# Sparse attention into a gated feed-forward layer: a new order in the lead-in, smaller weight loads, a finer first output stage and paired scores

## The chip, the cores and the metric

The kernel runs on one core of one Trainium2 chip. The metric is the time of one execution on the device in microseconds (us); where several executions were measured, their median. Each profile shows one execution. Its engines are TensorE (PE for matrix products, PEld for the loads of their stationary operand), VectorE (DVE), ScalarE (ACT), GpSimd (POOL) and SyncE (SP); the last two issue nearly all DMA transfers.

## What is computed

Attention over 4 batches, 8 heads, 768 positions and 64 dimensions. Each query sees the keys closer than 16 positions, and a maximum of the keys over each block of 32; the values of a block are averaged. The result, as 3072 rows of 512, goes through a feed-forward layer of width 2048.

```python
k_sum = k.reshape(B, H, nb, block, D).max(axis=3)        # block = 32
v_sum = v.reshape(B, H, nb, block, D).mean(axis=3)
scores_l = scale * q @ k.T,  masked to |i - j| < 16
scores_s = scale * q @ k_sum.T + log(block)
a = softmax(concatenate([scores_l, scores_s]))
x = (a @ concatenate([v, v_sum])).transpose(0, 2, 1, 3).reshape(3072, 512)
h = x @ w_in                                             # 512 x 2048
out = (h * sigmoid(1.702 * h)) @ w_out                   # 2048 x 512
```

## The kernel before, in words

**Units of work.** A batch is cut into two halves of 384 positions (`HALF`), a half into three stripes of 128 (`JH`). Heads go in pairs, numbered 0 to 3, so that a pair fills 128 partitions; two pairs form a group g. The feed-forward width is cut into 16 tiles of 128 (`NT`), numbered nt.

**Order.** Every engine executes its instructions in the order in which the program writes them (class `_Ordered`, lines 18 to 32). The order is written out by hand: in the lead-in as a list of calls (lines 895 to 1027), later as plans that say which piece of attention stands behind which slot of the feed-forward work. All instructions go through line 28, so the profile gives all of them that line; they are told apart by the names of the tiles.

**Lead-in** (lines 926 to 1005). Batch 0, first half, pair by pair. `k_turn` and `q_turn` transpose on TensorE (banks ps_k, ps_q); `k_max` takes the block maxima on DVE (ks); `s_bias`, `s_own`, `s_edges` make the scores (ps_s), `s_exp` their exponentials on ACT (a_sb). `b_turn(g)` makes the scores of the blocks for group g (ps_b, in two halves of two pairs of matmuls) from ks, `b_exp` their exponentials (ab). `v_sum(p)` sums the values of blocks (ps_vt), `v_copy` brings the sums to memory (vs). `av_own`, `av_edges` and `av_blocks` multiply with the values (ps_av), `v_norm` divides on DVE (rc, x), `x_turn` transposes the result (ps_x), `x_copy` copies it (xT), and `ff_first(p)` adds pair p's part to the first two tiles of the feed-forward layer (ph, lines 855 to 865). `gelu_soon` and `exp_soon` are one-element activations that make ACT load its table early.

**Loads** (lines 897 to 918, 1027). POOL issues them in the order of the program: queries, keys, values of batch 0, then w_in in five pieces of columns (256, 256, 512, 512, 512), w_out tiles 0 to 3, the late half of the queries (`load_q1`, four DMAs), w_out tiles 4 to 7 and 8 to 11, the masks (`finish_masks`, computed on POOL itself), w_out tiles 12 to 15, and then batch 1. At most eight DMAs of this queue are under way: an issue waits for the landing of the one eight places ahead of it.

**First output stage** (lines 1092 to 1099). `ff_out(0, ms, part)` multiplies stripe ms of the first half with four tiles of w_out (po). The twelve slots run over the four parts outside and the three stripes inside, so that a part of w_out is used by all stripes before the next is needed. Behind the slots, `plan0` (line 1030) puts the second half's attention of batch 0: q0 to q3 (`q_late`: transpose of the late queries of a pair into a bank, copy on DVE), s0 to s3 (`scores`, followed at once by `mask` on DVE), v0 and v1 (`values` of a group), x0 and x1 (`tx`, transpose and copy of the results). Behind slots 10 and 11, `w_sum(0)` and `w_sum(1)` make sums of w_out on DVE that later batches use. 

**Second half of batch 0, and batch 1.** `ff_in(1, ...)` with `todo` (line 1101) beside it: transposes of batch 1's keys (`tk`) and queries (`tq`), `w_sum(2)` and `w_sum(3)`, and `value_rows(1)` (block sums of batch 1's values, ps_vs). Then `ff_out(1, ms, part)` (line 1112, stripes outside, parts inside) with `plan1` (line 1032) beside it: t2, t3 (`tq`), s and m with half and pair (`scores`, `mask`), v with half and group, x with half and group, g (`gelu_soon`). Scores use the banks psb (two), values of batch 1, transposed queries, po and ph the banks pmm (four). Batches 2 and 3 follow plan `plan` beside sums and products of a fast matrix product (`product`, `g_sums`; poA, poB, poC).

**Last batch** (lines 1170 to 1221). Its feed-forward layer uses the same kind of fast product: `ff_do` runs seven products (1 to 7), copies (a, s, b, c) and gelus (A, B, C, E) for each j by the table `steps`, seven slots per j. Four tiles are computed plainly (`plain`). Banks: A three, B one, C two, E two. `x_sums` and `g_sums` are sums on DVE and POOL that the products use.

Of the kernel before, what the change touches and what calls it, by code (L numbers as in the profile page):

```python
# [10 lines left out]
BF16 = mybir.dt.bfloat16  # L11
# [24 lines left out]
def kernel(  # L36
# [225 lines left out]
    def load_w_out(c):  # L262
        wo = moe_w_out.rearrange("(nt ni) d -> ni nt d", ni=128)
        pool.dma_start(out=w_out_sb[:, c * 4:(c + 1) * 4, :],
                       in_=wo[:, c * 4:(c + 1) * 4, :])
# [151 lines left out]
    def q_late(p, eng):  # L417
        if p < 2:
            ps = psb.tile([128, 2048], BF16, name="ps_q", tag="big")
        else:  # L420
            ps = pmm.tile([128, 1024], BF16, name="ps_q", tag="mm")
        turn_plain(ps[:, 0:HALF], qb2["late"][:, 2 * p:2 * p + 2])
        copy(eng, qT[p][0][:, HALF:S].rearrange("p (c r) -> p c r", r=JH),
             ps[:, 0:HALF].rearrange("p (r c) -> p c r", r=JH))
# [206 lines left out]
    def tx(half, g):  # L631
        ps = psb.tile([128, 2, HALF], F16, name="ps_x", tag="big")
        for i in range(2):
            for j in range(JH):
                pe.transpose(out=ps[:, i, j * 128:(j + 1) * 128],
                             in_=x2[g][:, i, j].rearrange("p h d -> p (h d)"), identity=ident16)
        dve.tensor_copy(out=xTT[half][g], in_=ps)
# [231 lines left out]
    def ff_out(u, ms, part):  # L869
        if part == 0:  # L870
            po_now[ms] = pmm.tile([128, d_model], F32, name="po", tag="mm")
        po = po_now[ms]
        for nt in range(4 * part, 4 * part + 4):
            pe.matmul(out=po, lhsT=gT[u % 2][:, nt, ms * 128:(ms + 1) * 128],
                      rhs=w_out_sb[:, nt, :], start=(nt == 0), stop=(nt == NT - 1))
        if part == 3:
# [92 lines left out]
    b_turn(1)  # L969
    b_exp(1)  # L970
# [5 lines left out]
    av_edges(1)  # L976
    av_blocks(0)
# [8 lines left out]
    v_norm(2)  # L986
    v_sum((3,))
# [15 lines left out]
    x_copy(3, dve)  # L1003
    ff_first(2)
# [16 lines left out]
    for p in range(NP):  # L1021
# [18 lines left out]
    def beside0(slot):  # L1040
        for what in plan0.get(slot, ()):
            i = int(what[1])
            if what[0] == "q":
                q_late(i, dve)
            elif what[0] == "s":
                scores(0, 1, i)
                mask(1, i)
                if i == NP - 1:
                    gelu_soon()
            elif what[0] == "v":  # L1050
                values(0, 1, i)
            else:
                tx(1, i)

    def beside(b, slot):
        for what in (plan1 if b == 1 else plan).get(slot, ()):
# [44 lines left out]
    todo = {3: [lambda: tk(0, 1, act)], 4: [lambda: w_sum(2, 0)], 5: [lambda: tk(1, 1, act)],  # L1101
            6: [lambda: w_sum(2, 1)], 7: [lambda: w_sum(3, 0)], 8: [lambda: tk(2, 1, act)], 
            10: [lambda: w_sum(3, 1)], 9: [lambda: tq(0, 1, dve)], 11: [lambda: tk(3, 1, act)], 12: [lambda: tq(1, 1, dve)],
# [8 lines left out]
    for i, (ms, part) in enumerate((ms, part) for ms in range(JH) for part in range(4)):  # L1112
        ff_out(1, ms, part)
# [8 lines left out]
    for b in range(1, B - 1):  # L1122
# [5 lines left out]
        for n in range(0, NT, 2):  # L1128
# [12 lines left out]
            if nxt:  # L1141
                if n == 0 and b > 1:
# [47 lines left out]
    for i, tag in enumerate("CCE"):  # L1190
        plain(n * (i % 2), i // 2, tag)
# [60 lines left out]
```

## Time and profile before

| | us |
|---|---|
| median of 3 runs (lowest, highest) | 205.91 (205.42, 207.39) |
| the profiled execution | 205.23 |
| its span in the trace | 203.2 |
| TensorE busy | 197.0 |
| DVE busy | 141.0 |
| ACT busy | 125.4 |
| POOL busy | 90.6 |

| stretch of the span, us | what runs |
|---|---|
| 0 to 20 | lead-in |
| 20 to 30 | feed-forward input, first half of batch 0 |
| 30 to 44.7 | first output stage, second half of batch 0 beside it |
| 44.7 to 57.1 | feed-forward input, second half |
| 57.1 to 74.5 | output, second half, with batch 1's attention |
| 74.5 to 163 | batches 1 and 2, with the attention of the next batch |
| 163 to 203 | batch 3 |

A row of the timeline gives the start, the length, the engine, the line, the operation, the names of the tiles written and read, their shapes and the number of instructions that were merged; in brackets stands how long the engine had been idle and what ended that. PE lengths are modelled and overlap, so starts are safer than ends. The chain of waits goes back from the last instruction, at each step to what released it; it is shown in order of time.

### The profile page before, as it was taken

The page shows a single profiled execution, that of the slowest core. Times are in us where ns is not written, and L with a number is a line of the kernel's source. Part 1 is how long each engine was busy: PE and PEld are TensorE (multiplying, and loading weights), DVE is VectorE, ACT ScalarE, POOL GpSimd, SP SyncE. Part 2 cuts the span into 40 slices and gives each one's busy share as a digit, 9 for nine tenths or more (in the row PEclk, how much of TensorE's full clock was granted, in tenths as well). Part 3 has the DMA queues.
Part 4 walks back from the last instruction along what each step waited for, and adds up shares of the span by engine and source line. Part 5 has one row for each costly group of instructions (what it writes and reads, how often), then busy time and mean ns, then how long its engine had stood idle before and what let it go on. Part 6 is the DMA issues. An engine that isn't in the chain of part 4 may idle for free.

```text
span 203.2 us, 5849 instructions
## 1 busy us (share of the span) xinstructions
PE 197.0 (97%) x2358; PEld 136.8 (67%) x2358; DVE 141.0 (69%) x391; ACT 125.4 (62%) x240; POOL 90.6 (45%) x141
## 2 busy tenths in 40 slices
PE   6899999999999999999999999999999999999993
PEld 6557655556754566565888876656888856668882
DVE  6676884694856884898767789896769567758221
ACT  4674876539786717777871446778670568984220
POOL 7965489545999493001985046000000019870000
PEclk9999999999999999999999999999999999999999
DMA  6999999999999999999999979996022930000223
GB/s 177 165 166 204 207 210 215 187 157 239 109 136 165 179 178 176 116 156 160 128 180 153 176 136 137 191 212 135 0 106 60 187 117 3 0 0 0 106 105 103
DMA packets 95994, 28.13 MB, mean 138 GB/s; under 512 B 83664, under 2 KB 93152, under 8 KB 95968
## 3 DMA queue, kind: packets, MB, share of 16 engines
q0 software_dynamic: 69648, 13.24, 83.0%
q1 hardware_dynamic: 26176, 14.39, 34.2%
q8 instruction: 18, 0.29, 0.6%
q10 hardware_dynamic: 144, 0.13, 0.2%
q14 instruction: 8, 0.07, 0.1%
HBM read 27.26 MB, written 6.29 MB: 165 GB/s over the span
## 4 chain that ended last, share of the span: by engine, by line
PE 90%; DVE 4%; DMA 3%; ACT 1%; issue 1%; ACTq 0%; POOLq 0%; DVEq 0%
PE ph L28 32%; PE poA L28 16%; PE po L28 10%; PE poB L28 8%; PE ps_av L28 4%; PE phA L28 4%; PE poC L28 4%; PE ps_s L28 3%; DMA qe<-in_q_dram 3%; DVE ks L28 2%; PE ps_t L28 1%; PE ps_x L28 1%; DVE qT L28 1%; PE phB L28 1%; PE phC L28 1%; PE ps_q L28 1%
## 5 line engine op out<-in xcount | busy, mean ns | idle before, releaser
L28 PE MATMUL ph<-xT,w_in_sb 128*128 128x384 f16 x400 | 67.6, 326 | 0.1
L28 PEld LDWEIGHTS <-w_in_sb 128*128 128x128 f16 x442 | 42.7, 98 | 27.1 <-issue 0.2
L28 ACT ACTIVATE gT<-ph 128x384 f16<-128x384 f32 x100 | 47.8, 491 | 17.9 <-PE ph L28 17.1
L28 PEld LDWEIGHTS <-gT 128*128 128x128 f16 x312 | 28.8, 98 | 11.1
L28 ACT ACTIVATE a_sb<-ps_s 128x768 bf16<-128x768 f32 (+1 forms) x32 | 25.0, 826 | 11.6 <-PE ps_s L28 11.6
L28 PEld LDWEIGHTS <-gs 128*128 128x128 f16 x288 | 27.7, 98 | 3.4
L28 POOL DMA_DIRECT2D vw<-in_v_dram x36 | 24.5, 700 | 11.5 <-DMA kb<-in_k_dram 5.8
L28 POOL TENSOR_TENSOR gs<-gT 128x384 f16<-128x384 f16 x8 | 7.3, 907 | 42.6 <-PE phC L28 41.5
L28 PE MATMUL po<-w_out_sb,gT 128*128 128x512 f16 x96 | 23.6, 380 | 0.0
L28 DVE TENSOR_TENSOR a_sb<-a_sb,mk 128x768 bf16<-128x768 bf16 x28 | 14.8, 554 | 6.1 <-ACT a_sb L28 5.6
L28 PE MATMUL poA<-ws,gs 128*128 128x256 f16 x144 | 18.7, 273 | 0.0
L28 DVE TENSOR_TENSOR x<-ps_av,rc 128x384 f16<-128x384 f32 x32 | 17.8, 557 | 1.1
L28 DVE TENSOR_TENSOR gs<-gT 128x384 f16<-128x384 f16 (+1 forms) x34 | 13.2, 389 | 7.2 <-ACT gT L28 6.9
L28 POOL DMA_DIRECT2D qb<-in_q_dram x16 | 15.1, 967 | 2.2 <-DMA w_in_sb<-in_moe_w_in_dram 1.3
L28 PEld LDWEIGHTS <-kx 64*128 64x128 bf16 (+1 forms) x378 | 9.9, 95 | 7.3 <-issue 3.9
L28 POOL DMA_DIRECT2D kb<-in_k_dram x14 | 13.6, 988 | 0.3 <-issue 0.3
L28 DVE TENSOR_REDUCE ks<-kx 128x24 bf16<-128x768 bf16 x12 | 11.4, 948 | 3.4 <-ACT kx L28 3.2
L28 ACT ACT_TABLE_LOAD x10 | 12.8, 1283 | 1.0 <-PEq L1236 0.8
L28 ACT ACTIVATE osb<-poA 128x256 f32<-128x256 f32 x9 | 3.5, 383 | 15.8 <-PE poA L28 15.8
L28 ACT ACTIVATE s<-poA 128x256 f32<-128x256 f32 x11 | 4.2, 385 | 11.2 <-PE poA L28 11.2
L28 PEld LDWEIGHTS <-a_sb 128*64 128x64 bf16 (+2 forms) x400 | 7.8, 108 | 2.8 <-issue 1.7
L28 PE MATMUL poA<-w_out_sb,gT 128*128 128x256 f16 x72 | 9.4, 273 | 0.0
(117 smaller groups left out, 288.9 us busy)
## 6 DMA issues: line engine op xcount, KB each, us to landing
out_dram<-osb SPq DMA_DIRECT2D x22, 256.0 KB, 3.4
kb<-in_k_dram POOLq DMA_DIRECT2D x14, 192.0 KB, 6.5
qb<-in_q_dram POOLq DMA_DIRECT2D x12, 192.0 KB, 9.0
vw<-in_v_dram POOLq DMA_DIRECT2D x36, 64.0 KB, 5.1
w_out_sb<-in_moe_w_out_dram POOLq DMA_DIRECT2D x4, 512.0 KB, 13.0
w_in_sb<-in_moe_w_in_dram POOLq DMA_DIRECT2D x3, 512.0 KB, 12.4
vw<-vs SPq DMA_DIRECT2D x6, 198.0 KB, 7.0
gT<-in_k_dram SPq DMA_DIRECT2D x2, 384.0 KB, 3.4
```

The lines of the kernel that those rows point to most:

```text
L28: r = f(*a, **kw)
```

## The change

- **Weights:** w_in's third piece is cut in two (six pieces); w_out is loaded in pieces of two tiles up to tile 11 and one of four; three of its pieces come behind the masks, and the last.
- **Lead-in:** `b_turn(1)` and `b_exp(1)` go behind `av_edges(1)`; `x_turn(0)` ahead of `v_sum(3)`, `x_turn(1)` ahead of `av_blocks(3)`, `ff_first(0)` ahead of `x_turn(2)`, `ff_first(1)` and `ff_first(2)` ahead of `x_turn(3)`.
- **First output stage:** 24 slots of two tiles in place of twelve of four. `q_late` transposes the queries of two pairs into one allocation and copies them afterwards; all four pairs stand behind one slot. Masks are items of the plan. The sums of w_out move to `todo`, `w_sum(3)` to batch 1.
- **Batch 1:** s02 and s03, s10 and s11 stand in pairs; `tx` of half 0 copies on ACT.
- **Last batch:** the third plain group (half 1, tile 0) goes to slot 1, the fourth to slot 6 and another bank; `x_sums((3,))` behind the steps of slot 1.

```diff
-    def load_w_out(c):
+    def load_w_out(a, z):
         wo = moe_w_out.rearrange("(nt ni) d -> ni nt d", ni=128)
-        pool.dma_start(out=w_out_sb[:, c * 4:(c + 1) * 4, :],
-                       in_=wo[:, c * 4:(c + 1) * 4, :])
+        pool.dma_start(out=w_out_sb[:, a:z, :], in_=wo[:, a:z, :])
...
     def q_late(p, eng):
-        if p < 2:
-            ps = psb.tile([128, 2048], BF16, name="ps_q", tag="big")
+        if p == 0:
+            big, step = psb.tile([128, 2048], BF16, name="ps_q", tag="big"), 1024
         else:
-            ps = pmm.tile([128, 1024], BF16, name="ps_q", tag="mm")
-        turn_plain(ps[:, 0:HALF], qb2["late"][:, 2 * p:2 * p + 2])
-        copy(eng, qT[p][0][:, HALF:S].rearrange("p (c r) -> p c r", r=JH),
-             ps[:, 0:HALF].rearrange("p (r c) -> p c r", r=JH))
+            big, step = pmm.tile([128, 1024], BF16, name="ps_q", tag="mm"), HALF
+        both = [big[:, o:o + HALF] for o in (0, step)]
+        for i, ps in enumerate(both):
+            turn_plain(ps, qb2["late"][:, 2 * (p + i):2 * (p + i) + 2])
+        for i, ps in enumerate(both):
+            copy(eng, qT[p + i][0][:, HALF:S].rearrange("p (c r) -> p c r", r=JH),
+                 ps.rearrange("p (r c) -> p c r", r=JH))
...
-    def tx(half, g):
+    def tx(half, g, eng=dve):
...
-        dve.tensor_copy(out=xTT[half][g], in_=ps)
+        copy(eng, xTT[half][g], ps)
...
-    for n0, n1 in ((0, 256), (256, 512), (512, 1024), (1024, 1536), (1536, 2048)):
+    for n0, n1 in ((0, 256), (256, 512), (512, 768), (768, 1024), (1024, 1536), (1536, 2048)):
         load_w_in(n0, n1)
...
-    load_w_out(0)
+    load_w_out(0, 2)
+    load_w_out(2, 4)
     for a in range(NP):
         load_q1(a)
-    for c in range(1, 3):
-        load_w_out(c)
+    load_w_out(4, 6)
     finish_masks()
-    load_w_out(3)
+    load_w_out(6, 8)
+    load_w_out(8, 10)
+    load_w_out(10, 12)
+    load_w_out(12, 16)
...
     v_sum((0,))
-    b_turn(1)
-    b_exp(1)
     v_sum((1,))
     v_copy((0, 1), dve)
     av_own(0)
     av_own(1)
     av_edges(0)
     av_edges(1)
+    b_turn(1)
+    b_exp(1)
     av_blocks(0)
...
     v_norm(2)
+    x_turn(0)
+    x_copy(0, act)
     v_sum((3,))
     v_copy((3,), act)
     av_own(3)
     av_edges(3)
-    x_turn(0)
-    x_copy(0, act)
+    x_turn(1)
+    x_copy(1, act)
     av_blocks(3)
     v_norm(3)
-    x_turn(1)
-    x_copy(1, act)
+    ff_first(0)
     x_turn(2)
     x_copy(2, act)
-    ff_first(0)
+    ff_first(1)
+    ff_first(2)
+    x_turn(3)
     gelu_soon()
-    x_turn(3)
-    ff_first(1)
     x_copy(3, dve)
-    ff_first(2)
     ff_first(3)
...
-    plan0 = {1: ["q0", "q1", "q2"], 2: ["s0", "s1", "q3"], 4: ["s2", "s3"], 6: ["v0", "v1"], 8: ["x0"], 9: ["x1"]}
+    plan0 = {5: ["q0", "q2"], 8: ["s0", "s1", "m0", "m1"], 12: ["s2", "s3", "m2", "m3"], 17: ["v0", "v1"],
+             20: ["x0"], 23: ["x1"]}
-    plan1 = {-1: ["s00", "s01"], 1: ["t2", "m00", "m01"], 2: ["t3", "s02"], 3: ["s03", "m02"], 4: ["m03", "s10"],
-             5: ["s11", "m10"], 6: ["v00", "m11", "s12", "s13"], 7: ["v01", "g"], 8: ["m12", "m13"],
-             9: ["x00", "x01", "v10"], 10: ["v11"], 11: ["x10"]}
+    plan1 = {-1: ["s00", "s01"], 1: ["m00", "m01"], 2: ["t2", "t3"], 3: ["s02", "s03"], 4: ["m02", "m03"],
+             5: ["s10", "s11"], 6: ["m10", "m11", "s12", "s13"], 7: ["v00", "g"], 8: ["v01", "m12", "m13"],
+             9: ["x00", "v10"], 10: ["x01", "v11"], 11: ["x10"]}
...
-                tx(half, i)
+                tx(half, i, act if half == 0 else dve)
...
-    for i, (ms, part) in enumerate((ms, part) for part in range(4) for ms in range(JH)):
-        ff_out(0, ms, part)
+    for i, (ms, a) in enumerate((ms, a) for a in range(0, NT, 2) for ms in range(JH)):
+        ff_out(0, ms, a, a + 2)
         beside0(i)
-        if i in (10, 11):
-            w_sum(i - 10, 0)
-            w_sum(i - 10, 1)
...
+                if b == 1 and n in (8, 10):
+                    w_sum(3, n // 2 - 4)
...
-    for i, tag in enumerate("CCE"):
-        plain(n * (i % 2), i // 2, tag)
+    for i in range(2):
+        plain(n * i, 0, "C")
     x_sums(range(3))
...
         if slot == 1:
-            plain(n, 1, "B")
-            x_sums((3,))
+            plain(0, 1, "B")
+        if slot == 6:
+            plain(n, 1, "C")
             g_sums(0, pool, (0, 1, 2, 3))
         for j in range(PLAIN, n):
             for what in steps.get(slot - 7 * (j - PLAIN), ()):
                 ff_do(j, what)
+        if slot == 1:
+            x_sums((3,))
```

More of the change, by code (lines that the diff above doesn't have):

```diff
@@ L867, with ff_out @@
     po_now = {}
-    def ff_out(u, ms, part):
-        if part == 0:
+    def ff_out(u, ms, a, z):
+        if a == 0:
             po_now[ms] = pmm.tile([128, d_model], F32, name="po", tag="mm")
         po = po_now[ms]
-        for nt in range(4 * part, 4 * part + 4):
+        for nt in range(a, z):
             pe.matmul(out=po, lhsT=gT[u % 2][:, nt, ms * 128:(ms + 1) * 128],
                       rhs=w_out_sb[:, nt, :], start=(nt == 0), stop=(nt == NT - 1))
-        if part == 3:
+        if z == NT:
             osb = outp.tile([128, d_model], F32, name="osb", tag="osb")
@@ L1046, in beside0 @@
                 scores(0, 1, i)
-                mask(1, i)
                 if i == NP - 1:
                     gelu_soon()
+            elif what[0] == "m":
+                mask(1, i)
             elif what[0] == "v":
@@ L1093 @@
     beside0(-1)
-    for i, (ms, part) in enumerate((ms, part) for part in range(4) for ms in range(JH)):
-        ff_out(0, ms, part)
+    for i, (ms, a) in enumerate((ms, a) for a in range(0, NT, 2) for ms in range(JH)):
+        ff_out(0, ms, a, a + 2)
         beside0(i)
-        if i in (10, 11):
-            w_sum(i - 10, 0)
-            w_sum(i - 10, 1)
-    todo = {3: [lambda: tk(0, 1, act)], 4: [lambda: w_sum(2, 0)], 5: [lambda: tk(1, 1, act)],
-            6: [lambda: w_sum(2, 1)], 7: [lambda: w_sum(3, 0)], 8: [lambda: tk(2, 1, act)],
-            10: [lambda: w_sum(3, 1)], 9: [lambda: tq(0, 1, dve)], 11: [lambda: tk(3, 1, act)], 12: [lambda: tq(1, 1, dve)],
+    todo = {3: [lambda: w_sum(0, 0), lambda: tk(0, 1, act)], 4: [lambda: w_sum(0, 1)], 5: [lambda: tk(1, 1, act)],
+            6: [lambda: w_sum(1, 0)], 7: [lambda: w_sum(1, 1)], 8: [lambda: w_sum(2, 0), lambda: tk(2, 1, act)],
+            10: [lambda: w_sum(2, 1)], 9: [lambda: tq(0, 1, dve)], 11: [lambda: tk(3, 1, act)], 12: [lambda: tq(1, 1, dve)],
             15: [lambda: value_rows(1)]}
@@ L1112 @@
     for i, (ms, part) in enumerate((ms, part) for ms in range(JH) for part in range(4)):
-        ff_out(1, ms, part)
+        ff_out(1, ms, 4 * part, 4 * part + 4)
         beside(1, i)
```

## The prediction

> **What bounds the kernel now.** I read the page's shares first, then the chain of waits in order of time, then the timeline at each place where the chain leaves TensorE. The page:
>
> ```profile
> PE 197.0 (97%) x2358; PEld 136.8 (67%) x2358; DVE 141.0 (69%) x391; ACT 125.4 (62%) x240; POOL 90.6 (45%) x141
> DMA  6999999999999999999999979996022930000223
> ```
>
> TensorE is busy for 197.0 of 203.2 us, so an edit helps only where it removes a TensorE wait or TensorE work. The second row says that the DMA engines are full for the first 60% of the span: loads land at times that TensorE does not set, and a stage that comes early may find its data missing. Chain of waits, start and length in us:
>
> ```profile
> 60.27 0.86 PE po L28 x4
> ...
> 61.47 0.28 PE ps_s L28 x12
> 61.75 0.97 PE po L28 x4
> ...
> 167.01 0.58 DVE phB L28
> 167.63 0.48 PE phA L28 x2
> ```
>
> Two things are to be seen. Four po matmuls take 0.86 us behind work of their own array shape (60.27) and 0.97 behind a group of scores (61.75): a change of shape costs about 0.1, once in and once out. And there are a few waits on DVE and ACT, here in the last batch (167.01); the others follow below.
>
> **The lead-in.** Timeline of TensorE, then of DVE:
>
> ```profile
> 13.19 0.54 PE L28 MATMUL ps_vt<-v0n,E 128*128 128x64 bf16 x12
> 13.65 0.34 PE L28 MATMUL ps_b<-qT,ks 64*32 64x384 bf16 x2
> 14.38 0.34 PE L28 MATMUL ps_b<-qT,ks 64*32 64x384 bf16 x2 [0.39 <-DVE ks L28]
> 14.65 0.57 PE L28 MATMUL ps_vt<-v0n,E 128*128 128x64 bf16 x12
> ...
> 18.41 0.34 PE L28 MATMUL ps_x<-ident,x 128*128 128x128 f16 x3
> 18.59 0.34 PE L28 MATMUL ps_av<-vs,ab 128*128 128x130 bf16 x3
> 18.76 0.50 PE L28 MATMUL ps_x<-ident,x 128*128 128x128 f16 x6
> 19.33 0.48 PE L28 MATMUL ph<-xT,w_in_sb 128*128 128x384 f16 x2
> 19.81 0.34 PE L28 MATMUL ps_x<-ident,x 128*128 128x128 f16 x3
> 19.98 1.30 PE L28 MATMUL ph<-xT,w_in_sb 128*128 128x384 f16 x7
> ```
> ```profile
> 19.19 0.56 DVE L28 TENSOR_TENSOR x<-ps_av,rc 128x384 f16<-128x384 f32 x1
> 20.18 0.36 DVE L28 COPY xT<-ps_x 128x384 f16<-128x384 f16 x1 [0.44 <-PE ps_x L28]
> ```
>
> The second half of b_turn(1), at 14.38, waits for the block maxima of pair 3. With b_turn(1) moved behind av_edges, v_sum(1) follows v_sum(0) after 0.36 (13.65 - 13.19 less the change of shape), at 13.55 and not 14.65: 1.10 earlier. b_turn(1) comes back between av_edges and av_blocks, at two halves of 0.16 and one change of shape more, 0.42. So from av_blocks(0) on all is **0.68 early**. What is late next? The maxima are there (by 14.38) before b_turn(1) is reached, at about 14.9, and its exponential has v_sum(2) and two more groups to hide behind.
>
> From there the order differs. x_turn(0) (18.41 to 18.59: 0.18) now stands ahead of v_sum(3), and x_turn(1) ahead of av_blocks(3) where x_turn(0) stood. So av_blocks(3) starts at 18.59 - 0.68 + 0.18 = 18.09 and ends at 18.27 (0.17 to 0.18, as 18.59 to 18.76). ff_first(0) follows at once, since its copy is long done: two matmuls at 0.163 (1.30 for seven in the last row, less a tail of 0.16), to 18.60. There x_turn(2) starts. A turn, its copy on ACT and the first matmul that reads it take 19.33 - 18.41 = 0.92, so ff_first(2) starts at 19.52; x_turn(2) and ff_first(1) fill 0.5 of that, 0.4 is waiting. x_turn(3) stands behind ff_first(2), at 19.85. Its input is there: x ended 19.19 + 0.56 - 18.59 = 1.16 behind the start of av_blocks(3), so at 19.25. Turn and DVE copy take 20.18 + 0.36 - 19.81 = 0.73; with 0.04 for the hand-over (167.01 + 0.58 to 167.63 above) ff_first(3) starts at 20.63 and the first plain ff_in at 20.96. Before, ff_first(1) to (3) ran from 19.98 without a gap, to 19.98 + 6 x 0.163 = 20.96. **So the lead-in gives nothing**: the 0.68 is spent on two waits of 0.4 and 0.6, the second because ff_first(1) and (2) no longer cover the last turn. Ends: 0.7 faster if something else delays pair 3's turn before and not after, 0.4 slower if the value loads, which v_sum(1) now meets 1.1 earlier, come late. I take the middle because each term has its own row.
>
> **The weights in pieces.** POOL's timeline; a bracket names the landing that POOL waited for:
>
> ```profile
> 17.47 0.71 POOL L28 DMA_DIRECT2D qb<-in_q_dram  x1 [0.67 <-DMA w_in_sb<-in_moe_w_in_dram]
> 18.78 0.71 POOL L28 DMA_DIRECT2D qb<-in_q_dram  x1 [0.60 <-DMA w_in_sb<-in_moe_w_in_dram]
> 21.42 0.76 POOL L28 DMA_DIRECT2D w_out_sb<-in_moe_w_out_dram  x1 [1.92 <-DMA w_in_sb<-in_moe_w_in_dram]
> 23.92 0.74 POOL L28 DMA_DIRECT2D w_out_sb<-in_moe_w_out_dram  x1 [1.74 <-DMA w_in_sb<-in_moe_w_in_dram]
> 30.07 0.77 POOL L28 DMA_DIRECT2D w_out_sb<-in_moe_w_out_dram  x1
> 40.04 0.68 POOL L28 DMA_DIRECT2D vw<-in_v_dram  x1 [1.82 <-DMA w_out_sb<-in_moe_w_out_dram]
> ```
>
> In these rows an issue waits for the landing of the one eight places ahead. The second 256-column piece of w_in landed 1.31 behind the first (17.47 to 18.78), the 512-column piece 2.64 behind that (18.78 to 21.42): twice the bytes, twice the time, so a cut costs nothing that these rows show. Four more DMAs are 4 x 0.75 = 3.0 us of POOL issue, which moves the loads of batch 1 behind them; those join a queue whose last weights land near 40 (the last row), so that is hidden, and without that cover it is up to 3.0 late. The order of the bytes is unchanged, but the masks on POOL (24.66 to 30.07) now stand ahead of ten tiles of w_out, not of four. By 2.64 a piece back from 40.04, tiles 6 and 7 land near 34.8 and are used near 35.7; the later ones have more room. I take 0; ends 0 and 0.8 (second rival).
>
> The Trainium skill (DMA: Bandwidth & Descriptors, "Anatomy of one DMA") gives a DMA a fixed cost of about 2.0 us; paid in sequence, four more pieces would be 8 us. The trace disagrees for queued pieces: 1.31 for the half, 2.64 for the whole.
>
> **The first output stage.** The 48 po matmuls stay. By the two plans, changes of shape fall from nine to eight: 0.1. And a wait goes. Timeline of TensorE, then of ACT:
>
> ```profile
> 36.05 0.35 PE L28 MATMUL ps_s<-qT,kx 64*128 64x64 bf16 x12
> 36.55 0.35 PE L28 MATMUL ps_s<-qT,kx 64*128 64x64 bf16 x12 [0.15 <-DVE qT L28]
> ...
> 66.91 0.52 PE L28 MATMUL ps_s<-qT,kx 64*128 64x64 bf16 x24
> 67.36 0.82 PE L28 MATMUL po<-w_out_sb,gT 128*128 128x512 f16 x3
> ```
> ```profile
> 67.30 1.51 ACT L28 ACTIVATE a_sb<-ps_s 128x768 bf16<-128x768 f32 x2 [0.94 <-PE ps_s L28]
> ```
>
> Groups of a pair start 0.18 apart (two groups and a change of shape are 67.36 - 66.91 = 0.45); here it is 36.55 - 36.05 = 0.50, so 0.32 is waiting for the fourth query copy, which stood behind two masks on DVE. Now all four copies (at most 0.56 each, as the 19.19 row) start after slot 5, and the scores that need the fourth come seven slots of 0.43 later, 3 us against 2.3: covered. The next users have room as well: the second pair of scores comes 1.8 behind the first, against 1.51 for two exponentials, the values 2.2 behind the scores, the turns 1.3 behind the values. The sums of w_out move to DVE time in the next stage and in batch 1; DVE is busy 69% on the whole. **0.42 faster**; ends 0.1 and 0.5.
>
> **Batch 1's scores in pairs.** By the two plans the changes of shape fall from 17 to 14: 0.29 less. But s12 and s13 now follow s10 and s11 after one slot, and there are two score banks. With a pair starting at P, its exponentials run from P + 0.39 (66.91 to 67.30) to P + 1.90. The next pair starts at P + 0.45 + 0.97 = P + 1.42, its second group at P + 1.60, and needs the bank that comes free at P + 1.94. **A new wait of 0.34; the part costs 0.05.** Two copies of xT go from DVE to ACT, which has idle time there. Ends: 0.3 faster, 0.4 slower.
>
> **The last batch.** ACT's timeline, then TensorE's:
>
> ```profile
> 166.03 0.49 ACT L28 ACTIVATE gT<-ph 128x384 f16<-128x384 f32 x1 [0.53 <-DVE phC L28]
> 166.42 0.48 ACT L28 ACTIVATE vw<-phE 128x384 f32<-128x384 f32 x1
> ```
> ```profile
> 167.08 0.49 PE L28 MATMUL phE<-vw,kx 128*128 128x384 f16 x2
> ```
>
> phE's two matmuls are through at 167.08 + 0.33 = 167.41 and phA follows at 167.63: 0.22 of waiting for phB's addition, whose ACT copy (166.42) stood behind the gelu of 166.03. With plain(0,1) in that place the gelu comes a step earlier, and the plain group of slot 6 covers the addition; the wait goes. New: that group takes a bank of tag C, so j = 2's copy into C waits for a gelu; by the same kind of sum TensorE waits 0.05 for it. **0.17 faster**; ends 0.25 faster, 0.3 slower if it gets the other bank of C.
>
> **Sum:** 0.00 + 0.42 - 0.05 + 0.17 = 0.54 us less. What could eat it is the meeting with batch 2's values. The first row is SyncE's, whose copies wait for their landing, the second TensorE's:
>
> ```profile
> 79.80 2.70 SPq L28 DMA_DIRECT2D vw<-vw  x4
> ```
> ```profile
> 80.14 0.60 PE L28 MATMUL ps_vs<-vw,E 64*32 64x128 bf16 x48
> ```
>
> The sum over the values starts 0.34 behind the landing, and only its last sixth, some 0.3 later, reads the last piece: 0.64 of room. The 0.37 won by then fits, with 0.27 to spare.
>
> **Rivals.**
> 1. **Nothing on balance** (0.20): the new waits are larger than mine (banks in batch 1, the bank of C, pair 3's turn); 0.3 of loss in batch 1 and 0.1 in the last batch cancel the 0.42 of the first output stage: 205.9, as before. For it: the new orders leave the next waits 0.05 to 0.3 of room. Against it: the old waits were found by the same sums.
> 2. **Slower: the weight queue runs dry behind the masks** (0.10). While POOL makes the masks it has issued w_out only up to tile 5, which lands near 33.5; tiles 6 and 7 are issued at 30.07. Everything behind them shifts by d if they come later than 34.8. On an empty queue a first load took 5.47 (chain row below): 35.5, so d is 0.7; with SyncE's copies in the same engines I allow 2.0. It costs d - 0.27, so from d = 0.8 on the kernel is slower, and at 2.0 it takes 205.91 + 2.0 - 0.27 - 0.54 = 207.1. A cost per piece would act in the same place; the rows give it none, and I give it 0.02 of the 0.10. With the fixed cost that the page of the Trainium skill states it would be 8 late and 213.
>
> ```profile
> 1.38 5.47 DMA qe<-in_q_dram
> ```
>
> 3. **Faster by 1%** (0.07): all waits counted go and none takes their place: 0.68, 0.42, 0.29, 0.22, and 0.4 for the two waits on copies between 19.1 and 19.98, together 2.0: 203.9. Against it: the two waits around pair 3's turn follow from program order.
>
> **Numbers.** The profiled execution took 205.23 us (a span of 203.2 and 2.0 around it), 0.7 under the median of the runs shown, 205.91. The sum gives 204.69 for it and 205.91 - 0.54 = 205.37 for a median. The forecast, a gain of 0.2 to 1.0, has 0.63. About 1% is what a measurement here can tell from no change: faster by that 0.07 (third rival), slower 0.07 (most of the second), within it 0.86 (the forecast, the first rival, the rest). The range reaches from the third rival's end, 204.0, to 206.8, short of the second's.
>
> **What would show it.** Right: no gap between the first two groups of ps_vt; a wait of about 0.6 of the fourth pair's ph on a DVE copy of xT; none of ps_s on qT near 37; one of 0.3 of ps_s in batch 1 near 66; none of phA near 167. Wrong: po waiting for w_out, ps_vs for vw, or phC's copy for a gelu by over 0.3.

## The result, and the profile after

| | before | after |
|---|---|---|
| median, us (lowest, highest, runs) | 205.75 (205.32, 207.39, 6) | 208.31 (207.15, 209.43, 6) |
| the profiled execution, us | 205.23 | 208.25 |
| its span, us | 203.2 | 206.5 |

The ratio of the times is 1.0121, with a 95% interval of 1.0088 to 1.0153: the changed kernel is 1.2% slower. The prediction was 205.37 with a range of 204.0 to 206.8; it missed by 2.9 us, on the wrong side. Ratios here leave disturbed executions out, so that they can differ a little from the quotient of the medians. From the page of the changed kernel, the two rows that answer to those shown of before:

```profile
PE 197.4 (96%) x2358; PEld 137.2 (66%) x2358; DVE 140.8 (68%) x389; ACT 127.0 (62%) x242; POOL 92.8 (45%) x145
DMA  6999999999999999999999989999022940000223
```

TensorE has the same number of instructions and only 0.4 us more of work, for a span that is 3.3 us longer: the rest is waiting. The DMA row shows nothing of the cause: its slices are 5 us long and read 9 from 90% up. The page's row of what the engines moved does show it, in its seventh figure (about 31 to 36 us), 215 GB/s before and 138 after:

```profile
GB/s 177 165 166 204 207 210 215 187 157 239 109 136 165 179 178 176 116 156 160 128 180 153 176 136 137 191 212 135 0 106 60 187 117 3 0 0 0 106 105 103
```
```profile
GB/s 175 166 167 200 208 205 138 199 155 218 135 160 155 181 182 174 118 163 182 108 172 132 128 167 131 108 245 200 0 103 50 171 140 3 0 0 0 105 103 102
```

Where the 3.3 us arise is read from the starts of TensorE's groups in the two timelines (us):

| stretch, from the first of one group to the first of the next | before | after | difference |
|---|---|---|---|
| start to ps_vt | 13.19 | 13.44 | +0.25 |
| lead-in: ps_vt to the first plain ph | 7.77 | 8.54 | +0.77 |
| feed-forward input of the first half | 9.10 | 9.10 | 0 |
| first output stage: po to ph | 14.48 | 14.55 | +0.07 |
| second half's input, to its first po | 13.50 | 14.57 | +1.07 |
| its output with batch 1's attention | 16.47 | 16.56 | +0.09 |
| to batch 2's first product (poA) | 66.33 | 66.81 | +0.48 |
| batch 2's products | 22.02 | 22.02 | 0 |
| last batch to its first product | 17.77 | 17.91 | +0.14 |
| to the end | 22.60 | 23.04 | +0.44 |

**Lead-in.** TensorE's timeline after the change:

```profile
14.18 0.25 PE L28 MATMUL ps_av<-v0n,a_sb 128*128 128x65 bf16 x3
15.28 0.91 PE L28 MATMUL ps_av<-v0n,a_sb 128*128 128x65 bf16 x29 [0.85 <-issue]
...
19.89 0.48 PE L28 MATMUL ph<-xT,w_in_sb 128*128 128x384 f16 x2
20.56 0.48 PE L28 MATMUL ph<-xT,w_in_sb 128*128 128x384 f16 x2 [0.18 <-ACT xT L28]
20.88 0.33 PE L28 MATMUL ps_x<-ident,x 128*128 128x128 f16 x3
21.66 1.62 PE L28 MATMUL ph<-xT,w_in_sb 128*128 128x384 f16 x9 [0.45 <-DVE xT L28]
```

The gap between the first groups of ps_vt is gone, as predicted. But in the middle of a group that had begun, with the same operands, TensorE stops for 0.85 us on "issue": no semaphore is waited for. Then come the two predicted waits: two matmuls at 0.163 from 19.89 end at 20.22, and the next start is 20.56 (0.34; predicted 0.4); three turns from 20.88 end at 21.05, and the next start is 21.66 (0.61; predicted 0.6).

**Loads.** POOL's timeline after the change, then the one row of before that answers to its last:

```profile
24.39 0.70 POOL L28 DMA_DIRECT2D w_out_sb<-in_moe_w_out_dram  x1 [1.82 <-DMA w_in_sb<-in_moe_w_in_dram]
...
30.43 0.23 POOL L28 TENSOR_SCALAR_AFFINE_SELECT mk<-mk 32x64 bf16<-32x64 bf16 x1
30.61 2.88 POOL L28 DMA_DIRECT2D w_out_sb<-in_moe_w_out_dram  x4
...
42.62 0.69 POOL L28 DMA_DIRECT2D vw<-in_v_dram  x1 [2.37 <-DMA w_out_sb<-in_moe_w_out_dram]
...
57.68 0.74 POOL L28 COPY kx<-kx 128x80 bf16<-128x80 bf16 x3
```
```profile
54.88 0.74 POOL L28 COPY kx<-kx 128x80 bf16<-128x80 bf16 x3
```

The stretches of two microseconds, before and after; the last three columns are the granted clock, the share of the DMA engines and GB/s:

```profile
30.00:32.00 2.00, 2.00 (x14) 0.81 (x13) 0.17 (x1) 1.82 (x3) 2.00 (x4) 1.00 1.30 205
32.00:34.00 2.00, 2.00 (x48) 1.20 (x48) 1.49 (x3) 0.33 (x3) 2.00 (x3) 1.00 1.24 207
34.00:36.00 2.00, 2.00 (x14) 0.82 (x14) 1.09 (x3) 1.44 (x2) 2.00 (x3) 1.00 1.19 236
```
```profile
30.00:32.00 2.00, 2.00 (x13) 1.07 (x12) 1.20 (x7) 1.67 (x4) 1.89 (x5) 1.00 0.83 150
32.00:34.00 2.00, 2.00 (x17) 0.87 (x17) 0.00 (x0) 1.28 (x2) 2.00 (x4) 1.00 1.07 134
34.00:36.00 2.00, 2.00 (x33) 1.01 (x28) 1.67 (x4) 0.00 (x0) 2.00 (x3) 1.00 1.00 169
```

While POOL makes the masks it issues nothing, and at 30.61 only four transfers of its queue are still under way. The rate falls from 205 to 236 GB/s to 134 to 169 for six microseconds, and the last tiles of w_out land at 42.33 instead of 39.75. This is the second rival, 2.6 us late. TensorE's rows that pay for it and for the other differences:

```profile
42.38 1.46 PE L28 MATMUL po<-w_out_sb,gT 128*128 128x512 f16 x6 [0.46 <-DMA w_out_sb<-in_moe_w_out_dram]
...
59.91 0.35 PE L28 MATMUL ps_s<-qT,kx 64*128 64x64 bf16 x12 [0.71 <-POOL kx L28]
...
68.20 0.35 PE L28 MATMUL ps_s<-qT,kx 64*128 64x64 bf16 x12
68.72 0.35 PE L28 MATMUL ps_s<-qT,kx 64*128 64x64 bf16 x12 [0.18 <-ACT a_sb L28]
...
143.11 0.53 PE L28 MATMUL ps_s<-qT,kx 64*128 64x64 bf16 x24 [0.41 <-DMA qT<-qb]
...
168.52 0.48 PE L28 MATMUL phC<-xT,w_in_sb 128*128 128x384 f16 x2 [0.17 <-DVE phC L28]
```

At 42.38 the finer output stage waits for its last weights and loses what it had gained. At 59.91 batch 1's first scores wait for keys that POOL copies itself: these copies stand in POOL's order behind the issues of batch 1's loads, and each issue waits for an earlier landing, so a late queue makes them late too (57.68 against 54.88). At 68.72 stands the predicted wait of s13: 0.52 behind the group before it instead of 0.18, so 0.34. At 143.11 the last batch's queries come late, and at 168.52 the changed opening of the last batch waits for a copy of DVE.

### The profile page after: what moved, and what is told of

Read it like the earlier page. It is cut to its first block, busy times and chain, and to the rows that moved or that the text cites. A ratio compares the mean times of both kernels' runs of the same rounds, so it can differ in the third digit from the quotient of the medians.

```text
span 206.5 us, 5859 instructions
## 1 busy us (share of the span) xinstructions
PE 197.4 (96%) x2358; PEld 137.2 (66%) x2358; DVE 140.8 (68%) x389; ACT 127.0 (62%) x242; POOL 92.8 (45%) x145
## 3 DMA queue, kind: packets, MB, share of 16 engines
q1 hardware_dynamic: 26176, 14.39, 34.7%
## 5 line engine op out<-in xcount | busy, mean ns | idle before, releaser
L28 ACT ACTIVATE a_sb<-ps_s 128x768 bf16<-128x768 f32 (+1 forms) x32 | 24.7, 826 | 10.3 <-PE ps_s L28 10.3
L28 DVE TENSOR_TENSOR a_sb<-a_sb,mk 128x768 bf16<-128x768 bf16 x28 | 15.7, 584 | 7.8 <-ACT a_sb L28 7.0
```

The lines of the kernel that those rows point to most:

```text
L28: r = f(*a, **kw)
```

## The experiments

Fourteen kernels. Each gets the ratio to the kernel before on its own chip, with a 95% interval. The fourth column holds the lead-in from ps_vt to the first plain ph, the fifth the first output stage, the last the stretch from the last batch's first product to the end, all in us from the trace.

| kernel | median | ratio (interval) | lead-in | stage | end |
|---|---|---|---|---|---|
| before | 205.75 | 1 | 7.77 | 14.48 | 22.60 |
| after | 208.31 | 1.0121 (1.0088 to 1.0153) | 8.54 | 14.55 | 23.04 |
| e1_masks_early | 206.38 | 1.0022 (0.9999 to 1.0046) | 9.14 | 14.04 | 23.04 |
| e2_lead_old | 208.30 | 1.0112 (1.0075 to 1.0149) | 7.74 | 15.32 | 23.04 |
| e3_masks_lead | 205.96 | 1.0005 (0.9984 to 1.0025) | 7.96 | 14.03 | 23.04 |
| e4_loads_only | 209.40 | 1.0150 (1.0103 to 1.0196) | 7.83 | 14.52 | 23.06 |
| e5_bturn_only | 205.60 | 0.9986 (0.9956 to 1.0015) | 7.82 | 14.49 | 22.60 |
| e6_idle20 | 209.14 (one run) | | 8.30 | 14.04 | 23.05 |
| e7_pieces_only | 208.69 | 1.0136 (1.0079 to 1.0192) | 7.74 | 14.91 | 23.04 |
| e8_stage_only | 205.51 | 0.9981 (0.9948 to 1.0015) | 7.75 | 14.35 | 22.61 |
| e9_stage_masks | 206.12 | 0.9982 (0.9948 to 1.0016) | 7.75 | 14.03 | 23.04 |
| e10_old_last | 205.94 | 0.9987 (0.9956 to 1.0018) | 7.74 | 14.04 | 23.25 |
| e11_masks_mid | 207.81 | 1.0082 (1.0049 to 1.0115) | 9.42 | 14.03 | 23.03 |
| e12_masks_twice | 207.78 | 1.0048 (1.0007 to 1.0089) | 7.74 | 14.64 | 22.60 |
| e13_one_split | 206.34 | 1.0014 (0.9985 to 1.0043) | 7.75 | 14.39 | 22.81 |
| e14_pool_pad | 205.49 | 0.9981 (0.9955 to 1.0008) | 7.90 | 14.04 | 22.60 |

### First four: what the masks' place and the lead-in cost

**e1_masks_early**, on the changed kernel:

```diff
     load_w_out(2, 4)
+    finish_masks()
     for a in range(NP):
         load_q1(a)
     load_w_out(4, 6)
-    finish_masks()
```

> The changed kernel, with the masks on POOL moved ahead of the late queries' loads (behind w_out tiles 2 and 3); sizes and order of the loads as changed. Theory A (the weight queue ran dry behind the masks, from 30 to 36 us): the queue stays full, the last w_out piece lands near 40 instead of 42.3, po waits for no weights, the scores that open batch 1 wait for no key copy of POOL (1.0 us in the changed kernel), and the kernel is 1.0 to 1.8 us faster than the changed one, so about 0.3 to 0.6% slower than before. Rival B (every piece costs a fixed time on the queue): the last piece still lands 2 us later than before, and the time stays that of the changed kernel, 1.2% above before.

Its stretches:

```profile
32.00:34.00 2.00, 2.00 (x12) 0.88 (x9) 0.00 (x0) 1.80 (x3) 1.91 (x3) 1.00 1.24 204
34.00:36.00 2.00, 2.00 (x31) 1.13 (x30) 1.12 (x3) 0.00 (x0) 2.00 (x3) 1.00 1.24 208
```

The hole in the rate is closed, po waits for no weight, the scores for no key, and the time falls by 1.9 us to 1.0022 of before. The stage takes 14.04, a gain of 0.44 where 0.42 was predicted.

**e2_lead_old**: the changed kernel with before's list of calls from the first `v_sum` to `ff_first(3)`.

> The changed kernel with the lead-in's list of calls as before. Theory S (in the new order TensorE reaches instructions that have not been fetched yet, and waits 0.9 at 15.3 us; then two waits around pair 3's turn): the idle time of 0.85 at 15.28 goes, the first plain ff_in starts near 21.1 instead of 21.98, and the kernel is 0.7 to 1.0 us faster than the changed one, unless the loads take that back. Rival (what I predicted, the two orders are worth the same): ff_in still starts near 21.9, no change.

The lead-in is back at 7.74 with no stop on "issue". The time stays at 1.0112: TensorE comes earlier and waits longer for the same late weights (the stage takes 15.32, with waits of 0.4 and 1.1 for w_out), and the second half's output starts at 60.18 against 60.20. While the queue is late, the lead-in is worth nothing.

**e3_masks_lead**: both edits together.

> Both of these edits in one kernel; the first output stage, batch 1 and the last batch stay as changed. Theories A and S, if their parts add: 2.0 to 2.6 us faster than the changed kernel, 0 to 0.4 faster than before. If the loads are the only bound behind the lead-in: no faster than the kernel with the early masks alone.

1.0005: the two together account for the whole loss.

**e4_loads_only**: the kernel before with the changed kernel's loads (finer pieces, masks behind w_out tiles 4 and 5) and nothing else.

> The kernel before with nothing but the new load order (pieces of w_in and w_out, masks behind tile 5 of w_out). Theory A: the queue runs dry as in the changed kernel; po waits about 1 us near 38 for tiles 8 to 11, batch 1 opens late, and the kernel is 1.5 to 2.5 us slower than before, most of the whole loss. Rival (the loss comes from the lead-in and the plans): within 0.5 us of before.

1.0150: the order of the loads alone costs about as much as the whole change (the two intervals overlap). It is not paid where I expected: po waits for no weight, and the stage takes 14.52. The keys are late, so that the second half's first po comes 2.10 later in its stretch than before, and the stretch behind it takes 18.15 instead of 16.47. In that stretch of the profiled execution TensorE's granted clock was halved for some 3 us, behind waits of 0.56 and 0.70 us for keys:

```profile
62.00:64.00 2.00, 2.00 (x11) 1.05 (x9) 0.02 (x1) 0.00 (x0) 2.00 (x3) 0.50 1.06 210
```

So a part of the loss in this execution is a slower clock and not the late loads themselves; why the clock fell was not tested.

### The stop in the lead-in

**e5_bturn_only**, on the kernel before:

```diff
     v_sum((0,))
-    b_turn(1)
-    b_exp(1)
     v_sum((1,))
...
     av_edges(1)
+    b_turn(1)
+    b_exp(1)
     av_blocks(0)
```

> The kernel before, with one edit: the edge half of the second pair's keys (b_turn(1), b_exp(1)) goes behind av_edges(1), as in the changed kernel; the rest of the lead-in, the loads and all later stages are before's. Theory S (the removed wait was the cover of TensorE's own instruction supply): the first own values of the lead-in (ps_av) stop for about 1 us on 'issue', with no semaphore, at the same instruction as in the changed kernel, so the first plain tile of the hidden layer starts at 20.9 to 21.3 us (before 20.96): 0 to 0.3 us later than before, and the time is 205.7 to 206.4. The prediction's own step (the wait is gone and 0.68 us are had): no such stop, the first plain tile starts at about 20.3, and the time is 205.1 to 205.4.

**e6_idle20**, on the changed kernel:

```diff
-    idle(28)
+    idle(20)
```

> The changed kernel with 20 instead of 28 of the warming matmuls that open TensorE's program (they compute nothing that is used). Theory S (the stop of 0.85 us in the first own values is TensorE waiting for its next block of instructions, whose place is counted from the program's start): the stop moves by exactly eight matmuls, from the fourth matmul of the group to the twelfth, and starts some 0.4 us later by the trace. Rival V (the stop is a late load or copy, such as the natural values v0n, which landed at 15.01 us, whose wait the trace does not show): it stays at the fourth matmul. The time tells little here: 208.0 to 208.8.

TensorE in e5_bturn_only, then in e6_idle20:

```profile
13.76 0.25 PE L28 MATMUL ps_av<-v0n,a_sb 128*128 128x65 bf16 x3
14.77 0.91 PE L28 MATMUL ps_av<-v0n,a_sb 128*128 128x65 bf16 x29 [0.76 <-issue]
```
```profile
14.91 0.51 PE L28 MATMUL ps_av<-v0n,a_sb 128*128 128x65 bf16 x11
16.02 0.66 PE L28 MATMUL ps_av<-v0n,a_sb 128*128 128x65 bf16 x21 [0.60 <-issue]
```

With that edit alone the stop is there, at the same place, and nothing is gained: 7.82 against 7.77. With eight matmuls fewer at the program's start it stands behind the eleventh matmul of the group and not the third: eight later. So the place is counted in instructions (it is the 224th matmul of the program in each kernel with the stop), and a late load is ruled out. The trace also shows a transfer of 16 KB of instructions (its queue q8) that ends 1.24 to 1.44 us ahead of the first matmul behind the stop: at 13.92 in the changed kernel, 14.54 in e1_masks_early, 13.51 in e5_bturn_only, 14.78 in e6_idle20 and 14.66 in e11_masks_mid. In the kernel before it ended at 13.55, and the 224th matmul started at 15.04: the wait for the block maxima had just hidden the stop. By the 1.24 us above it could have started at 14.79 at the soonest, so moving that wait away leaves 0.25 at most. Kernels with before's own order bear this out: where the transfer ends later, the same matmul is held up there too, by 0.2 in e3 and e14 (ends at 14.32) and by 0.1 in e4 (14.03). In e3 it lengthens the second group of ps_vt, 0.57 before:

```profile
14.98 0.75 PE L28 MATMUL ps_vt<-v0n,E 128*128 128x64 bf16 x12
```

In none of the sixteen traces does this matmul start sooner than 1.2 us behind the end of that transfer.

### Pieces or masks

**e7_pieces_only**: the kernel before with all finer pieces, and the masks behind w_out tiles 10 and 11.

> The kernel before with the changed kernel's finer pieces of w_in and w_out, but with the masks where before has them in bytes: behind w_out tiles 10:12, ahead of the last piece only. Theory A (what costs is POOL's masks ahead of too many unissued pieces, not the pieces): the queue has work until the last piece, w_out tiles 4 to 11 land within 0.5 us of before's 37.24, the last at 39.5 to 40.5; span and time as before, 205.6 to 206.2. Rival B (each further piece costs by itself): five more pieces make the late queries, w_out and all behind later by 1 us or more and the time is 206.9 to 209.

**e12_masks_twice**: the kernel before, with a second `finish_masks()` behind the first.

> The kernel before, unchanged in its loads, but POOL writes the masks twice, so that it is busy with them for 11 us instead of 5.5 (the second writing gives the same masks). Theory Q: the queue holds 12.6 us when the masks begin and 11 + 4.6 are needed, so 3.0 lack: w_out tiles 12:15 land at 42 to 43.5 (39.75 before), the DMA engines' rate falls for 2 to 3 us near 37 to 40, batch 1's keys are late as in the changed kernel, and the time is 207.8 to 209.6. Rival B (finer pieces cost by themselves): no piece is changed here, so 205.7 to 206.3.

**e11_masks_mid**: the changed kernel with `finish_masks()` between the late queries and w_out tiles 4 and 5.

> The changed kernel with the masks one transfer earlier: behind the late queries, ahead of w_out tiles 4:6. Theory Q (POOL's queue holds eight transfers; the masks cost 5.5 us and a fresh transfer some 4.6 us from issue to landing, so the queue must hold 10.1 us of work when the masks begin; 12.6 before, 12.2 with early masks, 8.0 in the changed kernel, 6.9 with the masks latest): here the masks start at about 22.6 and the eighth transfer lands at about 31.9, so 9.3 are held and 0.8 lack: w_out tiles 12:16 land 0.5 to 1.2 us later than before's 39.75, and the time is between those of early masks (206.4) and of the change (208.3): 206.6 to 207.6. A cost per piece would leave it at 208.3; a place that only matters as early or late would leave it at 206.4 or 208.3.

In e7 I was wrong, and the time that I had given to the other theory came out, 208.69 (ratio 1.0136; the pieces are four more, not five as I wrote). The reason is in POOL's rows of e7 and in the stretch behind them; then the same stretch of e12:

```profile
29.52 0.69 POOL L28 DMA_DIRECT2D w_out_sb<-in_moe_w_out_dram  x1 [0.98 <-DMA w_out_sb<-in_moe_w_out_dram]
...
35.50 0.76 POOL L28 DMA_DIRECT2D w_out_sb<-in_moe_w_out_dram  x1
```
```profile
36.00:38.00 2.00, 1.42 (x29) 0.77 (x28) 1.64 (x4) 1.27 (x2) 2.00 (x3) 1.00 0.53 43
```
```profile
36.00:38.00 2.00, 1.70 (x30) 0.94 (x30) 1.28 (x3) 1.49 (x2) 2.00 (x3) 1.00 0.59 71
```

The queue is counted in transfers, eight, not in bytes. POOL came to the masks only at 30.20, when the eight still under way would last until 37.14, 6.9 us; the masks took 5.3, and the next transfer, issued at 35.50, landed at 41.60. So the hole lies at 36 to 38 with 43 GB/s, where before had 204. Finer pieces make the same eight places hold fewer bytes: 12.6 us of transfers when the masks begin before, 8.0 after. e12 shows the hole, 71 GB/s, with no piece changed, and the second half's first po comes 0.75 later in its stretch, with a wait of 0.58 for batch 1's keys; POOL's own longer work may share in that. Its size is below what I expected: the last tiles land 1.1 late (I had 2 to 3.7), and the ratio is 1.0048. In e11 they land 1.0 late, within the 0.5 to 1.2 expected, but its profile shows no wait of TensorE for a weight or a key; what it shows is a longer stop in the lead-in:

```profile
16.10 0.91 PE L28 MATMUL ps_av<-v0n,a_sb 128*128 128x65 bf16 x29 [1.72 <-issue]
```

So its time is in between, as expected (207.81, just above the 206.6 to 207.6 that I had), but the profiled execution does not give that loss to the loads, and e11 confirms no size. The direction of the theory stands (what the eight transfers hold when the masks begin must last until the next one behind the masks lands); my sum of 10.1 us that must be held is too coarse for a size.

A rule per piece is out: with the masks early all finer pieces are there and w_out is in by 39.34 (e9), 39.63 (e3) and 40.32 (e1), against 39.75 before. The Trainium skill, on the page DMA: Bandwidth & Descriptors, section Anatomy of one DMA — SWDGE (gpsimd) path, gives each DMA a fixed cost of about 2 us. These runs show no such charge on each piece of a full queue; the single transfer issued at 30.61, beside four others, took 4.6 us to land, which leaves room for such a delay but does not measure it.

### The parts that should gain

**e8_stage_only**: the kernel before with the finer first output stage only.

> The kernel before with the changed kernel's first output stage alone: 24 finer slots, the late queries turned in one group, masks apart from the scores, and the sums of weights that this stage held moved to the places they have in the changed kernel; lead-in, loads, batch 1's order and the last batch are before's. Theory (the prediction's step, seen so far only together with other parts): the stage from the first po to ff_in(1) takes 14.0 to 14.1 us instead of 14.48, and the end keeps that: 205.3 to 205.6, span 202.7 to 202.9. Rival (given back): batch 1's keys, copied by POOL behind its loads, or batch 2's values, are not earlier than before, so what the stage gains is waited away at ff_out(1) or at the first products, and the time is 205.8 to 206.1.

The stage gained 0.13 and not 0.44, and the last batch's queries were late in the profiled execution:

```profile
34.03 1.46 PE L28 MATMUL po<-w_out_sb,gT 128*128 128x512 f16 x6 [0.18 <-DMA w_out_sb<-in_moe_w_out_dram]
...
141.43 0.53 PE L28 MATMUL ps_s<-qT,kx 64*128 64x64 bf16 x24 [0.87 <-DMA qT<-qb]
```

The finer stage asks for w_out tiles 4 and 5 a little ahead of their landing in one piece with 6 and 7. It needs finer pieces.

**e9_stage_masks**: e8 with all finer pieces and the masks early.

> The kernel before with the two parts that the earlier runs found sound: the first output stage in finer steps, and the weights in finer pieces with the masks moved up behind w_out tiles 2:4 (where the queue held 12.2 us of transfers at their start in the run with this place). Lead-in, batch 1 and the last batch are before's. Theory: the first output stage takes 14.0 to 14.1 us (14.48 before; 14.35 with the coarse pieces, whose tiles 4:8 came 0.24 us late for it), nothing waits for a weight, and the first key copies of POOL start no later than before's 54.88 + 0.3, so ff_out(1) comes 0.2 to 0.5 us earlier than before: 205.2 to 205.6. Rival (given back at batch 3): its queries land just at their use in several runs (0 to 0.9 us of wait at 141); then the time is 205.6 to 206.4 though the stages up to 140 are ahead.

The stage takes 14.03, but the second half's output takes 16.85 (16.47 before and in e8) and the end 0.44 longer than in e8, and the ratio is the same 0.998.

**e10_old_last**: e3 with before's opening of the last batch.

> The changed kernel with the masks early, before's lead-in and before's last batch: against the run with the first two alone (205.96 us) only the last batch's opening differs. From the last batch's first ph to its first product went 17.77 us before and 17.91 to 18.28 with the changed opening. Theory (the changed opening loses: a copy of DVE stands behind sums that wait for the last queries' transfer): 17.7 to 17.85 here, and the time is 205.5 to 205.9. The prediction's step (the changed opening gains 0.17): 18.0 to 18.3 here and 206.0 to 206.3.

The opening takes 17.78 us, against 18.28 in e3 and 17.91 in the changed kernel; 17.77 or 17.78 is what every other kernel with before's opening has but e9 (17.89). DVE's rows of the changed kernel say why:

```profile
166.96 0.56 DVE L28 TENSOR_TENSOR vw<-xT,vw 128x768 f16<-128x768 f16 x1 [0.82 <-DMA xT<-x]
167.44 0.55 DVE L28 TENSOR_TENSOR vw<-xT,xT 128x768 f16<-128x768 f16 x1
167.91 0.56 DVE L28 COPY phC<-phA 128x384 f32<-128x384 f32 x1
```

The copy of 167.91, for which TensorE waits at 168.52, stands on DVE behind sums that wait 0.82 for the landing of xT, the transposing transfer of the attention's result (not of the queries, as I had written). The ratios of e10 and e3 don't tell 0.1 to 0.5 us apart.

**e13_one_split**: e8 with w_out tiles 4 to 7 in two transfers and the masks behind tiles 0 to 3. **e14_pool_pad**: e9 with eight repeated small writes among the masks.

> The kernel before with the finer first output stage, and of the finer pieces only the one that this stage misses: w_out tiles 4:8 in two transfers (one more transfer in all, where the change has four more); the masks stand behind w_out tiles 0:3, where the queue holds 14.7 us by the trace of before (14.53 to 29.26). Everything else is before's. Theory Q with theory F (the kernel's end takes 0.44 us longer in all ten profiled runs with all the finer pieces, 23.04 instead of 22.60 from the last batch's first product, by where POOL's last instructions fall in its stream) or theory D (by the number of transfers): the stage takes 14.0 to 14.1 us (14.48), no load is late, the end stays at 22.60 under F, and is 22.6 to 22.8 under D; the time is 205.2 to 205.6, ratio 0.996 to 0.999. Rival (the stage's gain is always given back before the end): 205.9 to 206.2.

> The kernel with the finer stage, all the finer pieces and the masks early (206.12 us), and eight more small writes of POOL among the masks, each repeating one that is made anyway; the transfers are the same. Theory F (the 0.44 us at the kernel's end hangs on where POOL's last instructions fall in its stream): the end takes 22.60 from the last batch's first product, as in the kernels without the pieces. Theory D (it hangs on the number of transfers): it stays at 23.04. The writes take some 1.6 us of POOL at a place where 12.2 us are held and 5.5 + 1.6 + 4.6 = 11.7 are needed, so no load should be late under either; the time is 205.4 to 206.3.

e14 has the same transfers as e9 and ends like the kernels without them: 22.60. So the 0.44 us at the end is not a price of transfers; it goes with the number of POOL's instructions. The trace has 195 of them before, 196 in e13, 207 in e14 and 215 in e12, all without it, and 199 in each of the ten kernels with it. The trace places it between POOL's last clearing of semaphores and the drain behind it: 0.03 us apart before, 0.32 after, and the drain takes 0.20 instead of 0.05. That the instruction supply is behind it here too is argued, not shown. The end of e13, 22.81, still missed the 22.60 of theory F: POOL's last steps are as before there, but an addition on DVE for the output starts late and costs TensorE 0.21. The same 0.21 is in e10's 23.25; its cause stays open. e13 also shows that one split is not enough: tiles 8 to 11, still one piece, are waited for at 37.07, and the stage takes 14.39; its time, 206.34, is above the 205.2 to 205.6 that I expected. In e14 the gain is met by batch 1's queries:

```profile
60.86 0.49 PE L28 MATMUL ps_t<-wide,qb 128*128 128x128 bf16 x6 [0.86 <-DMA qb<-in_q_dram]
```

So no version was measured to beat the kernel before: e5, e8, e9, e10 and e14 lie at 0.998 to 0.999, all with intervals that reach over 1.

## Why the prediction was wrong, step by step

- **Weights in pieces, taken at 0: wrong, and the main loss.** The prediction named the mechanism as its second rival, gave it 0.10, and let the lateness be 0.7, at most 2.0; it was 2.6, and loads in this order alone cost 1.5% (e4). Two steps failed. It said that tiles 6 and 7 would be the late ones and took an empty queue's latency for them, 35.5; they landed at 35.19, so that was right (tiles 4 and 5 at 33.09). But it took the pieces behind them to be late by no more than these, and they came 2.2, 1.6 and, for the double one, 3.3 us apart (37.41, 39.04, 42.33). The first of these lies in the stretch at 134 to 169 GB/s; why the double one took 3.3, where before's 512 KB pieces came 3.2 and 2.5 apart, no run isolates. And the price was set as d - 0.27 in one place, while the lateness is paid twice: 0.5 in the first output stage and 1.07 in batch 1's keys, which POOL copies behind issues that wait. The sum asked what lands late, and not what else waits behind POOL.
- **"From av_blocks(0) on all is 0.68 early": wrong.** The removed wait was there, and went; TensorE went on only 1.24 to 1.44 us behind a transfer of its instructions (e5, e6), so at most 0.25 of the 0.68 was to be had. The two waits that were to use up the 0.68 came as predicted, 0.34 and 0.61, so the lead-in lost 0.77 instead of nothing.
- **First output stage, -0.42: right** where the weights are there (0.44 in e1, e3, e9), lost in whole or in part where they are not (after, e8).
- **Batch 1's pairs, +0.05: right.** The wait of s13 is 0.34 as worked out, the stretch 0.09 longer.
- **Last batch, -0.17: wrong**, +0.14 in the changed kernel. The old wait of 0.22 is gone. The new one is not the bank of tag C for which the sum held 0.05, but DVE's copy behind the sums that wait for xT.
- **Not in the sum at all**: the 0.44 at the end. The 0.25 at the start is no part of the change: it is -0.2 to 1.1 in kernels whose TensorE instructions are equal up to there. Nor can the 0.48 at batch 2's first product be put down to it: the same wait cost 0.3 in e5 and 0.9 in e8, whose loads are before's.

## What to carry to other kernels

Cutting loads into finer pieces shortens what a queue of fixed depth holds; if the engine that issues them also computes, ask how long the transfers under way last when it turns away, and what else of its own work stands behind issues that wait. A wait that a profile shows may be the cover of another that it doesn't show: before counting on its removal, look for what arrives just in time behind it, the instructions included. A mechanism that is named as a rival with its rows should be priced through all its users before it gets a small chance.

## What the runs showed of the hardware that was not expected

**TensorE stops at a place that is counted in instructions.** It stood still for 0.60 to 1.72 us in the kernels that reached its 224th matmul early, and went on 1.24 to 1.44 us behind the end of a transfer of instructions. That it waits for that transfer follows from the times alone; making the transfer earlier was not tried.

**The first 10 us run at two speeds.** The same twelve turns of the first keys, in the changed kernel and in the kernel before:

```profile
4.78 0.85 PE L28 MATMUL ps_k<-wide,kb 128*64 128x128 bf16 x12 [0.31 <-ACT kb L28]
```
```profile
4.81 0.53 PE L28 MATMUL ps_k<-wide,kb 128*64 128x128 bf16 x12 [0.35 <-ACT kb L28]
```

TensorE's programs are the same up to there, and the idle time ahead of the turns is nearly so. In e9 and e10 the slow stretch lasted longest, and ps_vt came 1.1 us later than before; in e5 0.2 earlier. The Trainium skill, on the page TensorE: Matmul & The Clock Gate, section What's actually happening, says that the clock is decided in a window that runs freely and does not begin with the kernel. That agrees with these rows. The row of granted clock on the page shows full speed here all the same. The trace's list of clock changes tells why: it begins with a change to full speed, at 4.33 us before, at 7.05 in the changed kernel and at 10.3 and 10.6 in e9 and e10, and the row takes the time ahead of the first entry for full speed. In e1 the change comes at 5.06, within the twelve turns, and they take 0.60. For the comparison of profiles it means: count a lead-in from the first group behind this stretch, as the tables above do.
